# A written-out order of 831 operations replaced by another: same operations, other places, engines and buffers

## The chip, the cores and the metric

One core of a Trainium2 chip. The metric is the device time of one execution in microseconds (us). The core has the engines PE (matrix multiply), DVE (vector), ACT (activations and copies), POOL (general, no access to PSUM), and SP, whose queue issues nearly all DMAs here. They run on their own and wait for one another by semaphores; each works through its instructions in order. DMAs run on 16 DMA engines.

## What is computed

Attention over 32 inducing points, and behind it a mixture of experts with one expert per token (cut):

```python
B, N, C = 4, 11456, 128          # m = 32 inducing points
def mab(q, kv):                  # s = softmax(scale * q kv^T);  s @ kv
    ...
h = mab(I, x)                    # B x 32 x 128
x = mab(x, h)                    # B x N x 128, then rows as tokens
logits = xn @ en.T / tau         # xn, en: rows over their norms; E = 8
expert_idx = np.argmax(logits, axis=1)
gate_w = probs[np.arange(N), expert_idx]
out[mask] = gate_w[mask, None] * (np.maximum(x[mask] @ w1[e], 0.0) @ w2[e])
```

All in float32; `w1` is 8 x 128 x 1024, `w2` 8 x 1024 x 128.

## The kernel before

Each of the 4 batches is cut into 6 tiles of 1920 tokens (the last is shorter and padded), 24 tiles in all, numbered 0 to 23. A tile lies in SBUF as 128 x 1920, channels on partitions; stage 1 also needs it with tokens on partitions, which twelve tiles load from memory (`loadx`) and twelve make by transposes on PE (`xt`) and an eviction from PSUM (`xe`).

*Stage 1, per tile g* (line 380 on): `load`, the scores against the inducing points `s1` (PE), their exponentials `e1` (ACT), a 32 x 32 block transpose `e1t` (DVE), and `h`, 15 matmuls that add the tile to the batch's sum. *Per batch b* (`finish`, line 440 on): the sum of weights `zc`, `zr`, the scaled table row `rz` (which writes `rhs`), `hd`/`hdc`, the table `tab`/`tabc`, a `vote` and `pick` of the batch's expert, `loadw`, which loads that expert's weights, `tabs.0` to `tabs` (the expert's number, its one-hot row, the product with the table, its sum, and `tD`, the table less that sum; lines 481 to 484), `sta` to `std` (the shift of the exponent), and `G`, `GT`, `gs`, `gk`, `K`, `Kc`, `K4`, `K4c`, which fold the expert into a 128 x 128 matrix.

*Stage 2, per pair of tiles* (line 535 on): the scores `s2` (PE), their largest size `am` (DVE), exponentials `e2` (ACT), `rot` (a copy that turns the partitions by 32, two copies of 32 x 480 in each half), `up` (PE, 32 matmuls as run, half of them on `tD`), `uc`/`w` (weighting; on POOL for tiles 0, 2, 6, 14, 18 and 22, which `uc` copies out of PSUM first), `dt` (transpose), `n2` (norms), then small steps on 30 or 240 columns: `ln`, `ex`, `z`, `fac`, `den`, `lg`, `el`, `S`, `v`, `gf` (the gate). Per tile follow `F` (the gate spread out), `eg` (times the exponentials), `out` (PE), two evictions `oe` and the `store`. Tiles 18, 22 and 23 go through this last part in two pieces (`.0`, `.1`). At the end `ck1` to `ck5` and `verdict` decide on the core whether a general loop has to redo some batches; it runs for none here.

Nothing is scheduled while the kernel is built. The string `ORDER` lists all 831 operations; each engine gets its own in the order of that list. A quote behind a name takes the second engine of the operation's choices, two quotes the third:

```python
        for word in ORDER.replace("\n", " ").split(","):
            word = word.strip()
            o = named[word.rstrip("'")]
            o.engine = o.engines[len(word) - len(word.rstrip("'"))]
            assert o.deps <= done, o.name
            for b in o.bufs:
                if b.slot is None:
                    b.slot = int(next(seats[b.pool]))
```

`SEATS` gives each buffer its place as the list comes to it: 8 PSUM banks, 17 large SBUF buffers for tiles and outputs (`big`), 7 of middle size, 11 small ones, and so on. An operation waits for whoever used its place last. `FILL` puts matmuls on zeros in front of a few operations on PE. A load also waits for the fifth load before it (`DEPTH`). The line that writes all copies is L300, nearly all matmuls L303, transposes L406, the fill matmuls L708.

Of the kernel before, what the change touches and what calls it, by code (L numbers as in the profile page):

```python
# [23 lines left out]
F = 1024  # L24
# [8 lines left out]
K = 6  # L33
# [27 lines left out]
ind, en1, pad 5, en3, en4, load 0.1, xt 0.1, xe 0.1, en5, load 0.0, s1 0, load 1, en6, load 4, xt 0.0, xe 0.0, m1 0,  # L61
xt 1.1, sha 0, shb 0, xe 1.1, s1 1, shc 0, shd 0, en7, xt 1.0, xt 4.0, hde 0, e1 0, e1 1, xt 4.1, e1t 1, load 2, s1
2, xe 4.0, xe 1.0, e1 2, e1t 0, xt 2.0, xt 2.1, load 5, xt 5.1, pad 17, xe 2.0', e1t 2, h 0, xe 4.1, s1 4, h 1, load
3, xe 2.1, s1 3, h 2, e1 4, e1t 4, e1 3, e1t 3, xe 5.1', s1 5, loadx 3, xt 5.0, e1 5, xe 5.0, load 6, load 9, h 3,
zc 0, h 4, e1t 5, s1 6, h 5, hsb 0, m1 6, zr 0, sha 1, shb 1, load 11, xt 9.0, xe 9.0, rz 0.0, rz 0, hd 0, hdc 0',
shc 1, shd 1, s1 9, zk 0, tab 0, tabc 0', s2 0, vote 0, s2 4, am 0, sta 0, s2 2, pick 0, stb 0, tabs 0.0', tabs
0.1', stc 0, e1 6, load 7, am 4, e1 9, s2 1, tabs 0.2', tabs 0.3, std 0, load 10, e2 0, e1t 9, e2 4, tabs 0', am 1,
e2 1, s2 3, e2 2, load 12, am 3, rot 0.0, hde 1, s2 5, rot 0.1, e2 5, rot 4.0, e1t 6, up 0, s1 10, e2 3, am 2, am 5,
xt 10.0, loadx 6, uc 0, e1 10, load 8, ad 0, md 0, xe 10.0, rot 4.1, dt 0, up 4, mdc 0, xt 12.1, xe 12.1, w 1, w 4,
hde 2, xt 9.1, xe 9.1, loadw 0, dt 4, s1 7, xt 11.0, w 5, w 0, e1 7, xe 11.0, rot 2.1, z 0, n2 0, ln 0, ex 0, fac 0,  # L70
e1t 7, h 6, n2 4, ln 4, G 0, GT 0, s1 8, e1 8, up 2, e1t 10, loadx 7, gs 0, xt 10.1, den 0, gk 0, dt 2, s1 12, e1t
8, rot 2.0, loadx 8, h 7, lg 0, m1 12, z 4, ex 4, uc 2, marg 0.0, K 0, marg 0.1, el 0, sha 2, h 8, w 2, S 0, fac 4,
v 0, marg 0, shb 2, pad 11, Kc 0', s1 11, xe 10.1, mq 0, gf 0, den 4, w 3, n2 2, K4 0, shc 2, shd 2, lg 4, F 0, el
4, e1 11, S 4, v 4, e1t 11, xt 11.1, xe 11.1, F 1, mx 0, K4c 0', h 9, h 10, h 11, gf 4, zc 1, eg 0, F 5, ln 2, eg 1,
zr 1, z 2, hsb 1, ex 2, load 13, out 0, fac 2, rz 1.0, rz 1, hd 1, F 4, load 14, load 16, s1 13, e1 12, hdc 1', den
2, tab 1, e1t 12, eg 5, s2 6, tabc 1', vote 1, pick 1, s1 14, oe 0.1, lg 2, oe 0.0, out 1, el 2, S 2, eg 4, e1 13, v
2, tabs 1.0', e1 14, gf 2, am 6, sta 1, loadx 14, s2 9, tabs 1.1, tabs 1.2', s2 8, e1t 13, tabs 1.3, tabs 1, ad 1,
stb 1, oe 1.1, F 2, am 9, oe 1.0, stc 1, std 1, e2 6, s2 7, load 17, s2 11, am 8, eg 2', e2 9, rot 8.0, xt 17.0, e2
8, load 18, e2 11, am 7, ck1 0, e2 7, F 3, am 11, up 8, e1t 14, xe 17.0, eg 3, rot 8.1, s2 10, e2 10, rot 6.0, dt 8,
load 15, s1 15, e1 15, store 0, zk 1, up 6, rot 6.1, uc 6, h2 0, w 8, w 6, w 9, am 10, s1 16, e1 16, xt 12.0, dt 6,  # L80
n2 8, xe 12.0, out 2, w 7, md 1, loadw 1, G 1, mdc 1, xt 17.1, z 8, e1t 16, s1 17, rot 10.1, oe 2.1, n2 6, oe 2.0,
up 10, ln 6, GT 1, h 12, ex 6, z 6, fac 6, den 6, lg 6, ln 8, loadx 15, dt 10, xe 17.1, ex 8, el 6, S 6, gs 1, gk 1,
e1 17, fac 8, w 10, den 8, loadx 13, rot 10.0, h 13, out 3, h 14, w 11, K 1, oe 3.0, out 4, oe 3.1, e1t 15, h 15, Kc
1, K4 1, marg 1.0, e1t 17, oe 4.1, marg 1.1, marg 1, out 5, oe 4.0, lg 8, v 6, mq 1, mx 1, s1 18, zc 2, load 23, n2
10, gf 6, K4c 1, F 7, pad 23, m1 18, loadx 16, h 16, zr 2, rz 2.0, oe 5.0, h 17, oe 5.1, F 6, sha 3, rz 2, el 8, xt
18.0, S 8, hsb 2', hd 2, eg 6', v 8, ln 10, s1 23, z 10, shb 3, hdc 2', tab 2, store 1, ex 10, gf 8, loadx 19, shc
3, xe 18.0, F 9, tabc 2, shd 3, s2 17, e1 18, fac 10, eg 7', eg 9, vote 2, pick 2, s2 12, den 10, lg 10, e1 23, am
17, tabs 2.0', am 12, out 6, sta 2, el 10, tabs 2.1', oe 6.1, F 8, tabs 2.2', store 2, stb 2, s2 13, oe 6.0, zk 2,
stc 2, S 10, s2 16, std 2, e2 17, e1t 23, s2 15, v 10, am 16, gf 10', e2 12, e2 16, F 11, e2 13, am 15, rot 16.1,
out 7, eg 8, oe 7.0, oe 7.1, e2 15, eg 11, load 20, s1 20, e1 20, am 13, tabs 2.3, s2 14, tabs 2, F 10, am 14, eg  # L90
10, e2 14, e1t 18, rot 14.0, up 12, store 3, dt 12, rot 12.0'', up 14, uc 14, xt 18.1, rot 12.1, w 12, xe 18.1, dt
# [34 lines left out]
    sml=("0 1 2 1 0 2 2 1 0 8 3 5 2 4 3 5 3 2 5 0 4 8 1 0 6 9 1 5 8 4 3 2 10 7 8 1 2 5 7 6 4 5 7 4 2 1 0 8 5 7 9 6 "  # L126
        "2 0 9 10 0 8 10 1 8 9 4 5 2 8 10 5 9 7 3 8 2 4 3 2 5 7 8 4 5 6 3 4 6 5 0 10 5 4 "),
    E1=("0 1 1 1 0 1 1 0 0 1 1 0 1 1 0 0 1 1 1 0 0 0 1 1 "),
    gs=("0 1 0 1 0 0 1 0 1 1 0 1 "),
    b=("2 0 1 2 "),  # L130
    w=("0 0 0 0 "),
    k=("0 0 0 0 "),
# [746 lines left out]
```

## Time and profile before

| | |
|---|---|
| time of three runs | 163.42, 163.43, 163.44 us |
| the profiled execution's own time | 163.29 us |
| its span, from the first to the last instruction | 161.4 us |
| mean granted clock of PE | 0.988 |
| PE, DVE, ACT, POOL busy | 90%, 79%, 74%, 52% of the span |
| read from HBM, written | 39.47 MB, 23.46 MB |

The profile is one execution. A row of a timeline gives the start in the span, how long the instruction or a run of equal ones took, the engine and the line, what was written from what, and in brackets how long the engine had been idle and what released it. An engine off the chain of waits may be idle at no cost.

### The profile page before, as it was taken

To read this page: it belongs to the slowest core of one execution; us is meant where nothing else is said; L and a number is where in the kernel's file an instruction comes from. 1 tells how busy PE (TensorE), PEld (TensorE's weight loads), DVE (VectorE), ACT (ScalarE), POOL (GpSimd) and SP (SyncE) were. 2 spreads that over 40 slices of the span, in tenths; PEclk is the share of its full clock that TensorE was granted. 3 is DMA by queue.
4 is the path that set the end of the run, shared out by engine and by line. 5 is a ranking of instruction groups with operands and counts; after the bars stand their busy time and mean duration, and the time that the engine had idled before them with its cause. 6 is when DMAs were issued, how large, how long until landed. Compare 5 with 4: busy or idle time off the path is not lost.

```text
span 161.4 us, 5881 instructions
## 1 busy us (share of the span) xinstructions
PE 145.8 (90%) x2340; PEld 76.8 (48%) x2340; DVE 127.0 (79%) x300; ACT 119.8 (74%) x245; POOL 84.0 (52%) x200
## 2 busy tenths in 40 slices
PE   7899999999999999999999998999979888869930
PEld 5487777326658634255665323464822222335610
DVE  0515364697999789997979899999689979998970
ACT  3389372496967899688898998987979779988230
POOL 8600000259583862986305688932476987883300
PEclk9999999999999999999999999999999999999995
DMA  5999999999999999999999999999889999989993
GB/s 159 430 425 419 415 416 419 408 419 410 422 412 421 414 413 417 424 420 404 426 411 421 428 411 427 423 397 406 337 337 404 321 354 421 408 350 394 424 385 148
DMA packets 11295, 63.35 MB, mean 393 GB/s; under 512 B 1400, under 2 KB 1408, under 8 KB 11264
## 3 DMA queue, kind: packets, MB, share of 16 engines
q1 hardware_dynamic: 11088, 62.92, 96.3%
q8 instruction: 19, 0.31, 0.8%
q14 instruction: 12, 0.10, 0.2%
q10 hardware_dynamic: 176, 0.02, 0.1%
HBM read 39.47 MB, written 23.46 MB: 390 GB/s over the span
## 4 chain that ended last, share of the span: by engine, by line
PE 65%; DVE 19%; POOL 7%; issue 4%; DMA 2%; ACT 1%; POOLq 0%; DVEq 0%; ACTq 0%
PE psum L303 50%; PE psum L406 13%; DVE am L551 3%; DVE sml L624 2%; POOL mid L300 2%; POOL sml L626 2%; DVE n L589 2%; DMA emb_sb<-in_emb 2%; DVE big L300 2%; DVE mid L591 1%; DVE gf L611 1%; DVE mid L579 1%; DVE sml L626 1%; PE psum L374 1%; POOL mid L579 1%
## 5 line engine op out<-in xcount | busy, mean ns | idle before, releaser
L300 ACT COPY big<-psum 128x960 f32<-128x960 f32 (+4 forms) x71 | 62.3, 908 | 14.0 <-PE psum L303 7.9
L300 POOL COPY mid<-sml 32x480 f32<-32x480 f32 x46 | 27.4, 597 | 9.0 <-ACT sml L555 6.9
L303 PE MATMUL psum<-sml,K 32*128 32x480 f32 (+2 forms) x216 | 26.5, 564 | 3.6 <-ACT big L300 1.6
L303 PE MATMUL psum<-big,ind 128*32 128x480 f32 x192 | 25.0, 572 | 0.3 <-DMA big<-in_xT 0.3
L303 PE MATMUL psum<-big,sml 128*32 128x128 f32 x720 | 24.8, 274 | 0.2 <-issue 0.2
L303 PEld LDWEIGHTS psum<-big,sml 128*32 128x32 f32 x720 | 21.2, 110 | 5.9 <-issue 3.8
L406 PEld LDWEIGHTS psum<-ident,big 128*128 128x128 f32 x180 | 19.4, 140 | 9.1 <-ACT big L300 2.4
L406 PE MATMUL psum<-ident,big 128*128 128x128 f32 x180 | 23.5, 277 | 0.2 <-POOL sel L276 0.2
L303 PE MATMUL psum<-big,hd 128*32 128x480 f32 x192 | 22.4, 571 | 0.8 <-DVE mid L579 0.4
L626 POOL TENSOR_TENSOR sml<-mid,sml 128x480 f32<-128x480 f32 (+2 forms) x18 | 20.6, 1150 | 4.5 <-DVE sml L624 3.2
L425 ACT ACTIVATE E<-psum,nb 128x480 f32<-128x480 f32 (+2 forms) x28 | 18.3, 655 | 5.6 <-PE psum L303 4.6
L429 DVE STREAM_TRANSPOSE sml<-E 128x480 f32<-128x480 f32 x24 | 15.8, 661 | 4.9 <-ACT E L425 4.9
L624 DVE STREAM_TRANSPOSE sml<-gf 128x480 f32<-128x480 f32 (+2 forms) x27 | 16.1, 608 | 1.1 <-ACT gf L612 0.8
L551 DVE TENSOR_REDUCE am<-psum 128x1 f32<-128x480 f32 x24 | 15.1, 638 | 1.3 <-PE psum L303 1.0
L303 PEld LDWEIGHTS psum<-sml,K 32*128 32x128 f32 x216 | 8.8, 183 | 14.8 <-ACT big L300 3.8
L303 PE MATMUL psum<-mid,tab 32*32 32x480 f32 x96 | 13.7, 573 | 1.5 <-ACT mid L555 0.8
L589 DVE TRANSPOSE_TENSOR_REDUCE n<-mid 128x30 f32<-128x960 f32 x12 | 13.9, 1160 | 1.0 <-POOL mid L579 0.8
L591 DVE STREAM_TRANSPOSE mid<-psum 128x960 f32<-128x960 f32 x12 | 14.0, 1166 | 0.4 <-PE psum L303 0.2
L303 PE MATMUL psum<-sml,tD 32*32 32x480 f32 x96 | 12.9, 573 | 0.0
L303 PE MATMUL psum<-sml,tab 32*32 32x480 f32 x96 | 12.9, 573 | 0.0
L303 PE MATMUL psum<-mid,tD 32*32 32x480 f32 x96 | 12.9, 573 | 0.0
L579 DVE TENSOR_TENSOR mid<-psum,mid 128x480 f32<-128x480 f32 x18 | 11.2, 627 | 0.5 <-PE psum L303 0.3
(140 smaller groups left out, 210.2 us busy)
## 6 DMA issues: line engine op xcount, KB each, us to landing
big<-in_xT SPq DMA_DIRECT2D x19, 960.0 KB, 11.0
out<-big SPq DMA_DIRECT2D x14, 960.0 KB, 7.1
big<-in_xP SPq DMA_DIRECT2D x12, 960.0 KB, 11.6
w<-in_w SPq DMA_DIRECT2D x8, 512.0 KB, 8.6
out<-big SPq DMA_DIRECT2D x8, 512.0 KB, 7.8
big<-in_xT SPq DMA_DIRECT2D x4, 928.0 KB, 11.8
out<-big SPq DMA_DIRECT2D x6, 448.0 KB, 8.1
out<-big SPq DMA_DIRECT2D x2, 928.0 KB, 5.4
```

The lines of the kernel that those rows point to most:

```text
L300: return nc.scalar.copy(out, in_) if e == "ACT" else ENG[e].tensor_copy(out, in_)
L303: return nc.tensor.matmul(out, lhsT=lhsT, rhs=rhs, start=start, stop=stop)
L374: add(f"{name}a {bt.b}", ("PE",), lambda e: [nc.tensor.transpose(ap(p1)[0:1, 0:P], src(), ident)], [src_part, cnb], [p1])
L406: return [nc.tensor.transpose(ap(tp)[:, (q - q0) // 4, 128 * ((q - q0) % 4):128 * ((q - q0) % 4) + 128], v(q), ident) for q in range(q0, q1)]
L425: return [nc.scalar.activation(ap(e1)[r0:r1, :n], ap(ps)[r0:r1, :n], AF.Exp, bias=bt.t("nb")[r0:r1, 0:1], scale=SCALE, accum_out=bt.t("zk" ...
L429: add(f"e1t {g}", ("DVE",), lambda e: [nc.vector.transpose(ap(e1t), ap(e1))], [e1], [e1t])
L551: add(f"am {g}", ("DVE",), lambda e, ps=ps, k=k: [v.tensor_reduce(t("am")[:, k:k + 1], ap(ps)[:, :W], AX.X, ALU.max, apply_absolute_value= ...
L579: return [ENG[e].tensor_tensor(ap(wp)[:, a], src(), ap(e2)[:, a], ALU.mult)]
L589: add("n2 " + nm, ("DVE",), lambda e: [v.tensor_reduce(fl2(u("n2")), ap(wp).rearrange("p a (q i) -> p (a q) i", i=32), AX.X, ALU.add, appl ...
L591: add("dt " + nm, ("DVE",), lambda e: [v.transpose(ap(dt_).rearrange("p a q m -> p a (q m)"), ap(pd)[:, :, :W])], [pd], [dt_])
L624: add(f"F {nm}", ("DVE",), lambda e, a=a, f=f, q0=q0, q1=q1: [v.transpose(ap(f).rearrange("p (q i) -> p q i", i=32)[:, q0:q1], u("gf")[:, ...
L626: add(f"eg {nm}", ("POOL", "DVE"), lambda e, a=a, f=f, e2g=e2g, c0=c0, c1=c1: [ENG[e].tensor_tensor(ap(e2g)[:, c0:c1], ap(e2)[:, a, c0:c1] ...
```

## The change

`ORDER`, `SEATS` and `FILL` are replaced as a whole; no other line changes (the new file is one line shorter, so a line's number is one lower there). The words that come with it say that the new list was found by a search which charges the fetches of instruction pages to single transfer engines. All 831 operations are the same, and so are all sizes. 40 of them change engine: 12 from ACT to DVE, 9 from DVE to ACT, 8 from POOL to DVE, 7 from DVE to POOL, 3 from POOL to ACT, 1 from ACT to POOL. The fill matmuls go from 61 to 54.

```diff
 ORDER = """
-ind, en1, pad 5, en3, en4, load 0.1, xt 0.1, xe 0.1, en5, load 0.0, s1 0, load 1, en6, load 4, xt 0.0, xe 0.0, m1 0,
...
+pad 17, load 0.1, ind, xt 0.1, en1, en3, en4, load 0.0, en5, s1 0, m1 0, xt 0.0, xe 0.1, en6, en7', load 1, xt 1.1,
...
 FILL = {
-    "xt 0.1": (4, 16), "up 20": (7, 3), "up 22": (2, 4), "out 18.0": (5, 4), "out 23.1": (4, 30),
-    "out 23.0": (4, 4),
+    "xt 0.1": (0, 16), "K 3": (7, 6), "out 21": (2, 9), "out 23.0": (2, 23),
 }
```

On SP the stores and loads change places at several points. In the middle, `loadx 13` and `load 23` move some ten places forward, and `loadx 14`, `loadx 15` and `loadx 16` move behind `store 0`, `load 18`, `loadw 1` and `store 1`. `store 6` moves from behind the last load to ahead of the last three but one (`loadx 19`, `load 21`, `loadx 21`, `loadx 22` now end the loads).

DVE, at the choice of batch 3's expert. `g` and `ei` are the expert's number, `nb` the shift, `oh`, `lo` and `lg` the steps of `tabs`, `am` an `am`, the transposes `F`, the products of two tiles `eg`. Before:

```order
L467 MAX g_137<-psum 128x8
L467 MAX_INDEX ei<-g_137,psum 128x8
L377 COPY nb_127<-psum 128x1
L482 CAST idx_138<-ei 128x1
L624 STREAM_TRANSPOSE sml_80<-gf_99 128x480
L624 STREAM_TRANSPOSE sml_76<-gf_99 128x480
L483 TENSOR_REDUCE lg_140<-lo_139 128x1
L626 TENSOR_TENSOR sml_81<-mid_70,sml_83 128x480
L551 TENSOR_REDUCE am_125<-psum 128x1
L626 TENSOR_TENSOR sml_77<-mid_71,sml_76 128x480
```

After, at the same place:

```order
L466 MAX g_137<-psum 128x8
L466 MAX_INDEX ei<-g_137,psum 128x8
L376 COPY nb_107<-psum 128x1
L481 CAST idx_138<-ei 128x1
L481 TENSOR_SCALAR oh_109<-iota,idx_138 128x8
L482 TENSOR_TENSOR lo_139<-oh_109,tab_103 128x8
L482 TENSOR_REDUCE lg_140<-lo_139 128x1
L550 TENSOR_REDUCE am_105<-psum 128x1
L623 STREAM_TRANSPOSE sml_73<-gf_91 128x480
```

The one-hot row and the product have come over from POOL and follow the expert's number at once; the two `eg` (tiles 15 and 17) have gone to POOL.

POOL, over the same stretch of the program: `v` of pair 16, the `eg`, the steps of `tabs`, the `rot` of pairs 18 and 20 (copies of 32 x 480), `w 18`. Before:

```order
L608 TENSOR_TENSOR v_98<-sum_97,z_95 128x30
L626 TENSOR_TENSOR sml_78<-mid_70,sml_81 128x480
L482 TENSOR_SCALAR oh_129<-iota,idx_138 128x8
L483 TENSOR_TENSOR lo_139<-oh_129,tab_123 128x8
L300 COPY mid_68<-sml_82 32x480 x2
L484 TENSOR_SCALAR tD_124<-tab_123,lg_140 128x8
L300 COPY mid_68<-sml_82 32x480 x2
L300 COPY mid_66<-sml_75 32x480 x2
L579 TENSOR_TENSOR mid_69<-sml_76,mid_68 128x480
```

After:

```order
L607 TENSOR_TENSOR v_90<-sum_89,z_87 128x30
L625 TENSOR_TENSOR sml_80<-mid_66,sml_83 128x480
L625 TENSOR_TENSOR sml_78<-mid_70,sml_73 128x480
L299 COPY mid_71<-sml_81 32x480 x2
L483 TENSOR_SCALAR tD_104<-tab_103,lg_140 128x8
L299 COPY mid_71<-sml_81 32x480 x2
L625 TENSOR_TENSOR sml_74<-mid_67,sml_80 128x480
L578 TENSOR_TENSOR mid_70<-sml_75,mid_71 128x480
```

Two short steps have left POOL, `eg 12` and `eg 15` stand where `eg 14` stood, and `eg 17` has taken the place of a `rot` ahead of `w 18`.

PE, the last matmuls of the program (four `out` half tiles, 256 or 224 columns each, and the two transposes `ck2` and `ck4` of the check). Before, behind the first of the four:

```order
L303 MATMUL psum<-sml_83,K_128 128x256 x4
L303 MATMUL psum<-sml_77,K_128 128x224 x4
L658 MATMUL psum<-ident,chk 24x128
L660 MATMUL psum<-ident,c_160 1x24
L303 MATMUL psum<-sml_77,K_128 128x256 x4
```

After, all four:

```order
L302 MATMUL psum<-sml_81,K_108 128x256 x4
L302 MATMUL psum<-sml_74,K_108 128x256 x4
L302 MATMUL psum<-sml_74,K_108 128x224 x4
L302 MATMUL psum<-sml_81,K_108 128x224 x4
L657 MATMUL psum<-ident,chk 24x128
L659 MATMUL psum<-ident,c_160 1x24
```

The check's two transposes have moved behind the last output. Of the last eight evictions ACT has seven (five before) and DVE one (three before).

## Rows read from the trace of the kernel before

**Rows 1.** The page: engines over the span, and GB/s in 40 slices.
```profile
PE 145.8 (90%) x2340; PEld 76.8 (48%) x2340; DVE 127.0 (79%) x300; ACT 119.8 (74%) x245; POOL 84.0 (52%) x200
...
GB/s 159 430 425 419 415 416 419 408 419 410 422 412 421 414 413 417 424 420 404 426 411 421 428 411 427 423 397 406 337 337 404 321 354 421 408 350 394 424 385 148
```

**Rows 2.** Stretches: length, busy PE, PEld, DVE, ACT, POOL (instructions), PE clock, DMA share, GB/s.
```profile
4.50:116.40 111.90, 110.03 (x1928) 61.91 (x1928) 89.68 (x204) 87.97 (x187) 54.48 (x120) 1.00 1.01 415
116.40:157.50 41.10, 32.50 (x401) 12.69 (x400) 36.88 (x92) 30.58 (x58) 25.87 (x44) 1.00 0.96 376
```

**Rows 3.** Timeline of DVE behind stage 1: start, duration, instruction [idle before, releaser].
```profile
116.82 0.93 DVE L452 TENSOR_SCALAR rhs<-sel,zc 128x160 f32<-128x160 f32 x1
...
122.83 0.14 DVE L482 CAST idx<-ei 128x1 f32<-128x1 uint32 x1
...
124.10 0.12 DVE L483 TENSOR_REDUCE lg<-lo 128x1 f32<-128x8 f32 x1
...
130.01 1.18 DVE L589 TRANSPOSE_TENSOR_REDUCE n<-mid 128x30 f32<-128x960 f32 x1 [0.82 <-POOL mid L579]
...
144.50 1.17 DVE L589 TRANSPOSE_TENSOR_REDUCE n<-mid 128x30 f32<-128x960 f32 x1
...
149.36 0.69 DVE L611 RECIPROCAL gf<-v 64x30 f32<-64x30 f32 x2 [0.36 <-POOL v L608]
```

**Rows 4.** Timeline of POOL in the same stretch.
```profile
116.45 1.20 POOL L626 TENSOR_TENSOR sml<-mid,sml 128x480 f32<-128x480 f32 x1 [0.26 <-PE psum L303]
...
123.08 0.31 POOL L482 TENSOR_SCALAR oh<-iota,idx 128x8 f32<-128x8 f32 x1 [1.02 <-DVE idx L482]
...
123.75 1.53 POOL L300 COPY mid<-sml 32x480 f32<-32x480 f32 x2
125.39 0.76 POOL L484 TENSOR_SCALAR tD<-tab,lg 128x8 f32<-128x8 f32 x1
126.21 1.20 POOL L300 COPY mid<-sml 32x480 f32<-32x480 f32 x2
...
128.77 1.21 POOL L579 TENSOR_TENSOR mid<-sml,mid 128x480 f32<-128x480 f32 x1
```

**Rows 5.** Timeline of PE: most of `h 14`; the first matmul on `tD` of batch 3.
```profile
77.64 0.96 PE L303 MATMUL psum<-big,sml 128*32 128x128 f32 x27
...
126.20 0.58 PE L303 MATMUL psum<-mid,tD 32*32 32x480 f32 x1
```

**Rows 6.** Timeline of all engines, from 150 us to the end.
```profile
150.08 0.41 DVE L624 STREAM_TRANSPOSE sml<-gf 128x224 f32<-128x224 f32 x1
...
151.32 0.66 POOL L626 TENSOR_TENSOR sml<-mid,sml 128x224 f32<-128x224 f32 x1 [1.99 <-DVE sml L624]
...
151.78 0.97 ACT L300 COPY big<-psum 128x448 f32<-128x448 f32 x2 [2.50 <-PE psum L303]
...
152.78 4.28 SPq L639 DMA_DIRECT2D out<-big  x4
...
155.19 0.71 PE L303 MATMUL psum<-sml,K 32*128 32x256 f32 x8 [0.26 <-DVE fl L661]
...
155.97 0.59 ACT L300 COPY big<-psum 128x512 f32<-128x512 f32 x1 [1.77 <-PE psum L303]
...
157.33 0.14 DVE L679 CAST ni<-fw 1x1 int32<-1x1 f32 x1
```

**Rows 7.** A stretch behind PE's last matmul, columns as in rows 2.
```profile
155.90:157.40 1.50, 0.00 (x0) 0.00 (x0) 1.30 (x6) 0.59 (x1) 0.00 (x0) 1.00 0.97 384
```

**Rows 8.** SP's issues (`store 1`; the last two loads of batch 3).
```profile
63.94 2.02 SPq L639 DMA_DIRECT2D out<-big  x2
...
93.84 3.06 SPq L398 DMA_DIRECT2D big<-in_xP  x2
```

**Rows 9.** The twelve loads of line 398 (`loadx`), from issue to landing.
```profile
DMA to landing us min/median/max: 8.3/11.6/16.7
```

**Rows 10.** The page: the queue of the page fetches (packets, MB, share of 16 engines).
```profile
q8 instruction: 19, 0.31, 0.8%
```

## What I predict

> **What bounds the kernel now.** I read the profile in this order: the engines and the bytes per second of the whole span, the same split at the end of stage 1, the records of DVE, POOL and PE behind that point, and last the end of the program. [rows 1] show two resources near their limit: PE 90% busy, and a DMA rate over 400 GB/s in most slices, with a sag from slice 29 on. [rows 2] cut the span at 116.4 us, when `h 23`, the last matmul group of stage 1, is done. Ahead of the cut PE is busy for 110.03 of 111.90 us and the DMA share is 1.01: transfers and PE are both full, and PE's own idle time is 1.9 us in all. Behind the cut the DMA rate falls to 376 GB/s and PE is busy for 32.50 of 41.10 us, while DVE is busy for 36.88: there the stores wait for results. What follows is a chain that runs through batch 3's table and then its six tiles.
>
> **That chain, by its records.** Batch 3's table needs its row `rhs` (`rz 3`), which takes 0.93 us, while POOL runs an `eg` of 1.20 us beside it [rows 3, 4]. The expert's number is there at 122.97 (122.83 + 0.14). Then POOL makes the one-hot row (from 123.08) and the product, copies half a tile (`rot 18.1`, 1.53 us), and only then makes `tD` (0.76 us, to 126.15) [rows 4]. The matmuls on `tD` begin at 126.20 [rows 5], and with them `up 18`. POOL then has two more `rot` of 1.20 us ahead of `w 18`, which runs 128.77 to 129.98 [rows 4]; DVE's `n2 18` starts at 130.01, having waited 0.82 us for it [rows 3]. From there DVE is the row that never stops: `n2 22` at 144.50, the last gate `gf 22` at 149.36 [rows 3], and the last store is issued by 157.06 (152.78 + 4.28) [rows 6], the span ending at 161.4.
>
> **The change part by part.** No operation is added or taken away, so every cost is one of place.
>
> Ahead of the cut PE has the same 148 operations in front of `h 23`, in another order. Their sum is that of before, so `h 23` ends at 116.3 again unless PE waits more or less: at best 1.9 us earlier [rows 2], at worst by a late load (a rival below). I take 0, the row of the full engine being the nearest. SP now sends `store 6` ahead of the last three batch-3 loads: 0.98 MB at 415 GB/s, 2.4 us later. In before the last of these loads was issued by 96.90 (93.84 + 3.06) [rows 8]; with the median 11.6 us to landing [rows 9] and 2.4 us more it is there at 110.9, and its matmuls are among the last of stage 1, so it costs nothing; without that cover it would cost up to 2.4 us.
>
> Behind the cut I walk the new order with the durations of before's records. (1) `eg 13` now stands ahead of `v 14` on POOL, so it is over when `rz 3` starts; `rz 3` then takes about 0.3 instead of 0.93 us, of which the next operation on DVE takes nothing back, as `gf 14` has gone to ACT: -0.5. (2) `out 13` and `s2 18` follow on PE as before. `S 16` and `eg 14` on DVE come ahead of `am 18` and fit into the wait for `s2 18`: the shift is there at 122.1 instead of 122.92, -0.8. (3) The one-hot row, the product and the sum now follow on DVE itself, four short instructions of 0.12 to 0.3 us, 0.7 in all; the sum, at 124.22 in before (124.10 + 0.12 [rows 3]), is there at 122.8. POOL has `eg 12`, `eg 15` and `rot 18.1` ahead of `tD`: from `v 16` at about 120.7 three times 1.2 us gives 124.4, and `tD` is done at 125.1 instead of 126.15: -1.05. (4) `up 18` ends 1.05 earlier. Ahead of `w 18` POOL has `rot 18.0` and `eg 17`, again 2.4 us: 125.1 + 2.4 = 127.5, and `w 18` to 128.75: -1.2. `eg 17` on POOL is thus free, since it replaces `rot 20.1`, which moves behind. (5) `n2 18` starts at 128.8 instead of 130.01. On DVE up to `n2 22` the same sum is left within 0.2 us (`F 21` and `Kc 3` go out of the stretch, half of `eg 18` and `mdc 3` come in; the walk gives 143.45 for 144.50): -1.05. `lg 18` on POOL gains only 0.3, because `eg 16` and `z 20` now precede it; `gf 18` is still 1.1 earlier, as `den 20`, `am 22` and `Kc 3` ahead of it on DVE end last. (6) From `n2 22` to `gf 22` before needs 4.86 us. In after `F 21` is added and `oe 21.0` has gone to ACT; ACT's two evictions ahead of `el 22` set the pace in both, so 4.9: `gf 22` at 148.35, -1.0.
>
> At the very end two things trade. In before `out 22.0` stands behind `ck2` and `ck4` on PE and starts at 155.19, released by DVE's `fl`, so the last eviction on ACT starts at 155.97 after 1.77 us of waiting [rows 6]. Now the check follows the last `out`. Against that ACT makes seven of the last eight half evictions (five before), about 0.5 us each (0.97 for two [rows 6]), and `out 23.1` waits for `F 23.1` and POOL's `eg 23.1`. From `gf 22`: `F 23.0`, `F 22.0`, `eg 23.0`, `eg 22.0`, `F 22.1`, `oe 23.0.0`, `F 23.1` on DVE take 3.8 us with the gate (about 0.4 each [rows 6]; to 152.1), `eg 23.1` 0.66 behind `zk 3` (153.1), `out 23.1` 0.7 (153.8), two evictions 1.1 (154.9). The last two stores go out at 155.0 and 155.4, where before issued its last at 156.7: -1.3. They are two, of 0.43 and 0.46 MB, and land one behind the other, 0.3 us later than one would: -1.0. The check, thirteen steps of about 0.2 us, needs some 2.5 us behind `out 23.1`, which the eviction and the landing hide (before's last step of it is at 157.33 [rows 6], later than 156.4 here); if it were not hidden it would cost its excess over them.
>
> The `FILL` matmuls go from 61 to 54 and to other places. PE's granted clock was 1.00, the 2.4 GHz level, until 157.40, 1.5 us behind its last matmul [rows 7]; the gaps that the walk leaves on PE are under 1 us, so I count nothing. A gap that lets the clock fall would double some of the five `out` groups of 1.1 us on the way to the end.
>
> **The sum.** 161.4 - 1.0 = 160.4 us of span. The profiled execution took 163.29 us, 1.9 over its span, and lies 0.14 below the median of 163.43: 160.4 + 1.9 + 0.14 = 162.4 us. Bounds of the walk: -0.5, if only step 1 comes through and POOL keeps its pace, and -1.6, if the two last stores overlap and `lg 18` follows at once: 161.8 to 162.9.
>
> **Rivals.** *A load comes late ahead of the cut* (slower). `loadx 14`, `loadx 15` and `loadx 16` stood ahead of `store 1` on SP (which was issued at 63.94, for 2.02 us [rows 8]); now they stand behind it, and behind `store 0`, `load 18` and `loadw 1`, so that `loadx 14` is issued at 64 to 66. With the median of 11.6 us it is there at 75.6 to 77.6, with the longest, 16.7 [rows 9], at 80.7 or later. PE wants it for `h 14`, 77.64 in before [rows 5], now behind `K 1`, by an estimate 0.6 us later, at 78.3. For: this stretch of before has the long landings, and page fetches (19 packets, 0.8% of the engines' span [rows 10], so 1.1 us each on one engine) can hold a transfer up. Against: the order was laid out with such a hold-up in its sum, and no PE wait on a load is in before's trace beyond the start. Price 80.7 - 78.3 = 2.4 us on a full PE: 164.8 us. It decides from 1.0 us of waiting on, which eats the gain.
> The Trainium skill's page "Runtime: NRT & Kernel Launch" (Instruction fetch mechanics) says that a fetch of 16 KiB is mostly hidden; by it this rival would have no price and the sum would stay at 162.4. No row here shows whether a page fetch delayed a transfer.
>
> *The tail gains nothing* (same). POOL and DVE are both near full behind the cut [rows 2], and `rz 3`'s 0.93 us [rows 3] shows that one can stretch the other; if three more `eg` on POOL lengthen DVE's operations by as much as the table gains, the end stays: 163.4 us.
>
> *PE's idle time goes as well* (faster): 162.4 - 1.9 = 160.5 us. For: the waits that make it up are on ACT, DVE and a load, all of which moved. Against: a new order has new waits.
>
> *PE is not the limit ahead of the cut.* [rows 2] show PE busy for 110.03 but its weight loads for only 61.91 of 111.90 us. If PE could go faster there, `h 22` and `h 23`, at 0.96 us for 27 of a group's 30 matmuls [rows 5], could be done some 2 us behind the last load, at 112.9 instead of 116.3, and the end would be 3.4 us earlier still: 159.0 us. Against: no gap between matmul groups shows that they ever wait for the queue ahead.
> The Trainium skill's page "Perfetto Trace Analysis" (Identifying the Most-Contended Engine) holds matmul busy time for a bad measure and the weight loads' share for a better one; by that rule this rival is the case, but the trace shows a PE that takes up each group as the last one ends.
>
> **How the numbers follow.** Forecast 162.4 us, 47%; late load, 164.8 us, 26%; nothing gained, 163.4 us, 14%; idle time gone, 160.5 us, 10%; PE with room, 159.0 us, 3%. About 0.2% (0.33 us) is what a measurement of this kernel can tell from no change. Faster is the first, fourth and fifth: 60%; same 14%; slower 26%. The range 161.2 to 164.8 leaves out the lower part of the fourth case, the fifth, and late loads of more than 2.4 us, some 18%; the forecast's own range is 161.8 to 162.9.
>
> **What would show it.** Right: `h 23` done at 116.3 within 0.5 us; `tD` of batch 3 done near 125.1; `w 18` ending near 128.8; `gf 22` near 148.4; the last store issued near 155.4; the check's last step before the last landing. Wrong: idle time of PE ahead of `h 14` to `h 16` with a DMA named; `tD` still behind 126; a granted clock under 1.00 between 116 and 155 us; a DVE that is busy for as long behind the cut as before.

## The result: 0.8% faster, 161.95 us

The changed kernel takes 161.95 us (median of 20 runs, 161.37 to 163.64), the kernel before 163.44 us in the same series (20 runs, 162.98 to 164.51): a ratio of 0.9917, 95% interval 0.9897 to 0.9937. Forecast were 162.4 us, with a range of 161.2 to 164.8. Ratios and intervals, here and below, leave out executions over 1.5% above the fastest of their kernel (one each of e2, e7 and e10, two of e6); the medians count all. The traced execution took 162.65 us with a span of 160.9; it is one of the slower ones of the changed kernel, and the part on the late page names a cause that its trace shows.

The page of the changed kernel, the lines that answer to [rows 1] and [rows 10]:

```profile
PE 144.0 (90%) x2333; PEld 75.8 (47%) x2333; DVE 126.6 (79%) x306; ACT 119.6 (74%) x242; POOL 82.7 (51%) x195
...
GB/s 149 429 423 420 417 418 412 422 411 408 422 413 417 416 414 420 409 425 422 414 404 365 397 401 352 430 426 411 411 420 423 388 396 405 365 397 412 395 391 81
...
q8 instruction: 19, 0.31, 0.8%
```

The sag of slices 29 to 33 has gone: 411, 420, 423, 388, 396 for 337, 337, 404, 321, 354. In its place there are two new dips ahead of the cut, slices 22 and 25 with 365 and 352. The stretches of [rows 2], in the changed kernel:

```profile
4.50:116.40 111.90, 109.67 (x1923) 61.07 (x1923) 92.47 (x215) 85.64 (x179) 53.56 (x115) 1.00 1.02 412
116.40:157.50 41.10, 30.89 (x407) 12.48 (x397) 33.76 (x87) 32.69 (x63) 25.45 (x45) 0.96 0.99 398
```

Behind the cut 398 instead of 376 GB/s, and DVE busy for 33.76 instead of 36.88 us. The clock's mean of 0.96 comes from a fall at 154.5 us, 1.3 us behind the last output matmul; up to there it was 1.00. DVE along the chain, as [rows 3]:

```profile
116.78 0.17 DVE L451 RECIPROCAL zc<-psum 128x1 f32<-128x1 f32 x1 [0.45 <-PE psum L302]
116.98 0.37 DVE L451 TENSOR_SCALAR rhs<-sel,zc 128x160 f32<-128x160 f32 x1
...
122.69 0.68 DVE L481 TENSOR_SCALAR oh<-iota,idx 128x8 f32<-128x8 f32 x1
...
123.61 0.16 DVE L482 TENSOR_REDUCE lg<-lo 128x1 f32<-128x8 f32 x1
...
128.81 1.18 DVE L588 TRANSPOSE_TENSOR_REDUCE n<-mid 128x30 f32<-128x960 f32 x1
...
143.00 1.16 DVE L588 TRANSPOSE_TENSOR_REDUCE n<-mid 128x30 f32<-128x960 f32 x1
...
148.06 0.68 DVE L610 RECIPROCAL gf<-v 64x30 f32<-64x30 f32 x2 [0.28 <-POOL v L607]
```

`rz 3` takes 0.37 instead of 0.93 us, `n2 18` starts 1.20 us earlier (128.81 for 130.01), `n2 22` 1.50 us (143.00 for 144.50), the last gate 1.30 us (148.06 for 149.36). POOL in that stretch, as [rows 4]:

```profile
120.97 2.38 POOL L625 TENSOR_TENSOR sml<-mid,sml 128x480 f32<-128x480 f32 x2
123.42 1.22 POOL L299 COPY mid<-sml 32x480 f32<-32x480 f32 x2
124.75 0.32 POOL L483 TENSOR_SCALAR tD<-tab,lg 128x8 f32<-128x8 f32 x1
125.13 1.19 POOL L299 COPY mid<-sml 32x480 f32<-32x480 f32 x2
126.40 1.20 POOL L625 TENSOR_TENSOR sml<-mid,sml 128x480 f32<-128x480 f32 x1
127.57 1.20 POOL L578 TENSOR_TENSOR mid<-sml,mid 128x480 f32<-128x480 f32 x1
```

Two `eg`, `rot 18.1`, `tD`, `rot 18.0`, `eg 17`, `w 18` in one row without a gap: `tD` is done at 125.07 (126.15 before), `w 18` at 128.77 (129.98).

Two things made `tD` earlier. The first is the start of `rot 18.1`: it needs the exponentials that ACT makes with the shift, and starts 0.13 to 0.14 us behind them in all fourteen traces, whatever POOL did ahead of it. ACT before, ACT after, and POOL in e8 (an experiment below), which is idle ahead of the copy:

```profile
122.95 0.66 ACT L555 ACTIVATE sml<-psum,nb 128x480 f32<-128x480 f32 x1
...
122.63 0.66 ACT L554 ACTIVATE sml<-psum,nb 128x480 f32<-128x480 f32 x1 [0.27 <-DVE nb L376]
...
123.27 1.20 POOL L292 COPY mid<-sml 32x480 f32<-32x480 f32 x2 [1.23 <-ACT sml L547]
```

The second is that POOL's own steps got shorter: `rot 18.1` takes 1.22 instead of 1.53 us, `tD` 0.32 instead of 0.76. Before, DVE ran two `eg` beside them:

```profile
124.14 0.70 DVE L626 TENSOR_TENSOR sml<-mid,sml 128x480 f32<-128x480 f32 x1
...
125.33 0.64 DVE L626 TENSOR_TENSOR sml<-mid,sml 128x480 f32<-128x480 f32 x1
```

All four traces with the old tail (before, e1, e3, e9) have the second copy of `rot 18.1` at 0.91 us and `tD` at 0.76 to 0.77, all ten with the new one 0.58 and 0.31 to 0.32. Counted from DVE's first step behind `h 23` (RECIPROCAL of `zc`), `tD` is done 1.36 us earlier: 0.61 by the start of `rot 18.1`, some 0.75 by the two shorter steps. No run moved DVE's two `eg` alone, so that they stretch POOL's steps is read from these traces and not tested by itself.

The end, as [rows 6]: the last matmul group, SP's last two stores, the check's last step.

```profile
152.58 0.66 PE L302 MATMUL psum<-sml,K 32*128 32x224 f32 x8 [0.31 <-POOL sml L625]
...
154.30 0.84 SPq L638 DMA_DIRECT2D out<-big  x2
...
155.28 0.14 DVE L678 CAST ni<-fw 1x1 int32<-1x1 f32 x1
```

The stores are issued by 155.14 instead of 157.06, 1.9 us earlier, but by the packets of the trace the last of them lands at 158.54 instead of 159.31, only 0.8 earlier (by the semaphore that reports it 159.41 instead of 159.73, 0.3 earlier). The check is done at 155.42, 3.1 us ahead of the last packet (157.47 and 1.8 before).

### The profile page after: what moved, and what is told of

It reads as the page before. It is cut to its first block, busy times and chain, and to the rows that moved or that the text cites. A ratio compares the mean times of both kernels' runs of the same rounds, so it can differ in the third digit from the quotient of the medians.

```text
span 160.9 us, 5858 instructions
## 1 busy us (share of the span) xinstructions
PE 144.0 (90%) x2333; PEld 75.8 (47%) x2333; DVE 126.6 (79%) x306; ACT 119.6 (74%) x242; POOL 82.7 (51%) x195
## 4 chain that ended last, share of the span: by engine, by line
PE 59%; DVE 17%; POOL 6%; ACT 6%; DMA 4%; issue 3%; SPq 1%
PE psum L302 47%; PE psum L405 11%; DMA big<-in_xT 4%; DVE n L588 3%; ACT big L299 3%; POOL sml L625 3%; DVE mid L590 2%; DVE sml L623 2%; DVE sml L625 2%; DVE mid L578 1%; POOL mid L299 1%; ACT sml L554 1%; DVE big L299 1%; POOL lg L602 1%; ACT mid L554 1%
## 5 line engine op out<-in xcount | busy, mean ns | idle before, releaser
L302 PE MATMUL psum<-sml,K 32*128 32x480 f32 (+2 forms) x216 | 27.3, 566 | 5.8 <-ACT big L299 2.0
L625 POOL TENSOR_TENSOR sml<-mid,sml 128x480 f32<-128x480 f32 (+2 forms) x21 | 23.7, 1133 | 6.6 <-DVE sml L623 5.1
L299 POOL COPY mid<-sml 32x480 f32<-32x480 f32 x42 | 24.7, 588 | 3.7 <-ACT sml L554 1.7
L302 PE MATMUL psum<-big,sml 128*32 128x128 f32 x720 | 24.2, 274 | 0.0
L302 PE MATMUL psum<-mid,tab 32*32 32x480 f32 x96 | 13.0, 572 | 1.4 <-ACT mid L554 0.7
L602 POOL TENSOR_TENSOR lg<-mid,den 128x240 f32<-128x240 f32 x12 | 8.0, 665 | 9.9 <-DVE den L600 8.7
```

Source lines behind the costliest of these rows:

```text
L299: return nc.scalar.copy(out, in_) if e == "ACT" else ENG[e].tensor_copy(out, in_)
L302: return nc.tensor.matmul(out, lhsT=lhsT, rhs=rhs, start=start, stop=stop)
L602: add("lg " + nm, ("POOL",), lambda e: [gp.tensor_tensor(u("lg"), dv(), u("den").rearrange("p a q -> p q a").unsqueeze(3).broadcast_to([P, ...
L625: add(f"eg {nm}", ("POOL", "DVE"), lambda e, a=a, f=f, e2g=e2g, c0=c0, c1=c1: [ENG[e].tensor_tensor(ap(e2g)[:, c0:c1], ap(e2)[:, a, c0:c1] ...
```

## Experiments

All twelve against the kernel before, on the same chip as their own runs of it.

| label | what it is | median us | ratio | 95% interval |
|---|---|---|---|---|
| e1_front_only | new order to `h 23`, old behind | 162.96 | 0.9961 | 0.9940 to 0.9982 |
| e2_tail_only | old to `h 23`, new behind | 162.95 | 0.9960 | 0.9932 to 0.9988 |
| e5_tail_free_bank | the same, fills into free banks | 162.33 | 0.9907 | 0.9883 to 0.9931 |
| e3_b_check_last | before, check behind the last `out` | 163.93 | 1.0020 | 1.0002 to 1.0038 |
| e4_after_again | the changed kernel | 162.24 | 0.9921 | 0.9895 to 0.9947 |
| e6_page_shift | changed, 64 more instructions on PE | 163.54 | 0.9980 | 0.9960 to 0.9999 |
| e7_no_fill | changed, 38 of 54 fills left out | 162.57 | 0.9912 | 0.9879 to 0.9945 |
| e8_eg12_early | changed, `eg 12` earlier | 162.02 | 0.9902 | 0.9867 to 0.9936 |
| e9_before_late | before, 0.94 us behind `h 23` | 164.07 | 1.0035 | 1.0016 to 1.0053 |
| e10_after_late | changed, 0.94 us behind `h 23` | 162.62 | 0.9931 | 0.9904 to 0.9957 |
| e11_page_late | changed, 8 fewer on PE | 162.21 | 0.9912 | 0.9889 to 0.9936 |
| e12_best | e8 and e11 together | 161.96 | 0.9911 | 0.9878 to 0.9943 |

**Which half of the new order gains?** The list is cut behind `h 23`; the operations left follow in the order of the other list, and their buffers get free places that follow the parent's.

```diff
 e1: ORDER = new list up to "h 23"
-    + new list
+    + old list, without what stands ahead already (232 operations)
 e2: ORDER = old list up to "h 23"
-    + old list
+    + new list, without what stands ahead already (239 operations)
```

> The new order up to h 23, the old order behind it. My theory, that the gain lies behind h 23: h 23 done at 116.3 to 116.6 us, tD of batch 3 near 126.2, the last gate near 149.4, time 163.2 to 163.6 us, ratio 1.000. Rival, that the gain comes from the new place of loads and stores ahead of h 23 (fewer DMA gaps behind it because transfers are left over): 161.9 to 162.3 us, ratio 0.991 to 0.993.

> The old order up to h 23, the new order behind it. My theory: tD of batch 3 done near 125.0 us, w 18 near 128.7, the last gate near 148.4, time 161.9 to 162.4 us, ratio 0.991 to 0.994. Rival, that the gain lies ahead of h 23: 163.4 us, ratio 1.000. Second rival, that the two parts work only together: both this and the kernel with the new front stay at 163.0 us or above.

Both came out at 163.0: neither the theory nor its first rival, and the two halves seem to add up. The trace of e2 shows that its tail was not the one that I meant to run. Stretches of e2, columns as in [rows 2]:

```profile
144.00:146.00 2.00, 0.81 (x9) 0.04 (x4) 1.97 (x5) 1.60 (x6) 0.25 (x1) 1.00 1.03 412
146.00:148.00 2.00, 2.00 (x13) 1.19 (x13) 1.02 (x5) 1.20 (x2) 0.87 (x3) 0.54 1.02 404
148.00:150.00 2.00, 2.00 (x11) 0.67 (x12) 1.73 (x6) 0.13 (x1) 0.19 (x1) 0.61 0.99 402
```

And the timeline of PE there, fills and `out 21`:

```profile
145.99 1.97 PE L700 MATMUL psum<-zero 128*128 128x256 bf16 x9 [1.19 <-ACT big L292]
147.89 1.90 PE L295 MATMUL psum<-sml,K 32*128 32x480 f32 x8
```

The bank that my placing gave the fill in front of `out 21` was freed only by an eviction: PE idled for 1.19 us, the granted clock fell to the 1.2 GHz level, nine fills took 1.97 us and `out 21` 1.90 instead of 1.09. `out 23.0` began at 152.3, behind 23 fills of 2.69 us that began late in turn. The twelve times fall into two groups, 162.1 to 162.6 (six) and 163.3 to 165.6 (six); four of the six slower ones have a mean granted clock of 0.974 or less, the quicker ones none below 0.983. So it was run again with fills into banks that are free long before:

```diff
-FILL = {'xt 0.1': (4, 16), 'K 3': (7, 6), 'out 21': (2, 9), 'out 23.0': (2, 23)}
+FILL = {'xt 0.1': (4, 16), 'K 3': (4, 6), 'out 21': (0, 9), 'out 23.0': (2, 23)}
```

> Again the old order up to h 23 and the new one behind it, but the fill matmuls in front of out 21 and K 3 write to banks that are free long before. In the first such kernel the fill in front of out 21 waited 1.19 us for an eviction, PE's granted clock fell to 0.50 from 146 to 149.4 us and out 23.0 began at 152.3. My theory, that the tail is worth 1.0 us or more by itself and that the fallen clock ate the rest there: clock 1.00 to 152 us, out 23.0 near 149.9, time 162.1 to 162.5 us, ratio 0.990 to 0.994, and the runs no longer fall into two groups. Rival, that the tail is worth half and the front the other half: 162.9 us, ratio 0.996, whatever the clock does.

162.33 us, 0.9907: the new tail alone gives the whole gain, as far as the intervals tell. In the one traced execution the clock fell once more (0.50 from 142 to 146 us, behind 0.98 us of idle PE at 140.2), and that one took 163.23 us; the five others lie between 161.9 and 162.6. The part about the clock held by accident, then, rather than by the other bank; the size of the tail held.

What the two halves do to the chain can be read free of that, from DVE's first step behind `h 23` to `n2 22`, in us: before 28.00 (116.50 to 144.50), e1 28.05, e9 27.47; the changed kernel 26.22 (116.78 to 143.00), e2 26.65, e4 26.25, e8 26.20, e10 26.25. With the old tail it is 28 (27.5 in e9, for a reason that follows), with the new one 26.2 to 26.7 (27.3 in e5, where the clock had fallen), whatever stands ahead. Why the front gives 0.6 us with the old tail and nothing that can be measured with the new one is taken up with the delays.

**The end: check or store?**

```diff
-mx 3, oe 23.0.1, ck1 3, store 23.1, oe 23.0.0', ..., zk 3, ck2, store 23.0, ck3, ck4, ..., out 22.0, oe 22.0.0', ..., oe 22.0.1, store 22.0
+mx 3, oe 23.0.1, ck1 3, store 23.1, oe 23.0.0', ..., zk 3, out 22.0, oe 22.0.0', oe 22.0.1, ck2, store 23.0, ck3, ck4, ..., store 22.1, store 22.0, ...
```

> The old order, with one part of the new one: out 22.0 and its two evictions stand ahead of the check on PE, ACT and DVE. out 22.0 should start at 153.6 instead of 155.2 us and the last store be issued near 155.2 instead of 156.7. My theory, that transfers are full there (DMA share 0.94 to 1.01 from 152 to 158 us) and take back most of it: 0.3 to 0.6 us, time 162.8 to 163.1 us, ratio 0.996 to 0.998. Rival, that the issue of the last store alone sets the end: 1.3 to 1.5 us, time 162.0 us, ratio 0.991, which would be the whole of the gain. Rival, that the check is the end: no gain, 163.4 us.

0.2% slower, which none of the three had. The end of this kernel, PE and DVE:

```profile
155.29 0.71 PE L295 MATMUL psum<-sml,K 32*128 32x256 f32 x8 [1.10 <-DVE big L292]
...
156.90 0.37 PE L650 MATMUL psum<-ident,chk 128*24 128x128 f32 x1 [0.90 <-DVE big L292]
...
159.11 0.14 DVE L671 CAST ni<-fw 1x1 int32<-1x1 f32 x1
```

`out 22.0` now waits 1.10 us for a bank that DVE's eviction of another half tile holds, and the check, pushed behind it, ends at 159.25 (157.47 before; 0.63 us of that come from ahead of the cut). SP turns to the last store only 0.10 us later than before (156.82 for 156.72), but its last packet lands 1.35 us later (160.66 for 159.31).

Which of the two holds the end can be read from all fourteen traces. The span ends 1.6 to 2.5 us behind the last packet, and 1.25 to 1.67 behind the semaphore that reports the last store (1.46 to 1.49 in ten); behind the check's last step it is anything from 3.3 (here) to 5.6. In before that step has 3.9 us to the end, more than the 3.3 that are enough here, so it was the landing that held the end there too. So e3 lost by its landing: what the last store won by going ahead of the check the transfers took back, and more; why they took so much is not shown.

**How much do 0.94 us on the chain cost?** In both orders eight fills stand between `h 23` and `zr 3`:

```diff
 FILL = {
+    'zr 3': (1, 8),
```

> The kernel before with eight more fill matmuls (0.12 us each, 0.94 in all) between h 23 and zr 3, so that batch 3's table and all behind it begins 0.94 us later. The walk of the prediction says that the chain behind h 23 sets the end here: last step of the check and last landing each 0.9 us later, time 164.3 to 164.6 us, 0.8 to 1.0 above the kernel before. Rival, that the transfers set the end (DMA share 0.94 to 1.01 in the last 7 us): 0.5 us or less, 163.9 us or below.

> The changed kernel with the same 0.94 us between h 23 and zr 3. If the chain still sets the end: 162.9 to 163.1 us, 0.8 to 1.0 above the changed kernel. Theory, that the end now waits for transfers (its last landing is 3.1 us behind the last step of the check, in the kernel before 1.8; DMA share 0.97 from 116 to 157 us): the end moves by 0.3 to 0.6 us, time 162.4 to 162.6 us. That would also say why the new front, worth 0.6 us with the old tail, is worth less with the new one.

Before, delayed: 164.07 us, 0.59 above its own runs of before (163.48). That looks like part of the delay only, but the chain itself was only 0.52 us later (`n2 22` at 145.02). DVE and POOL in that kernel:

```profile
116.41 1.20 POOL L618 TENSOR_TENSOR sml<-mid,sml 128x480 f32<-128x480 f32 x1 [0.27 <-PE psum L295]
...
117.87 0.20 DVE L444 TENSOR_SCALAR rhs<-sel,zc 128x160 f32<-128x160 f32 x1
```

POOL's `eg 13` is over at 117.61, `rz 3` starts behind it and takes 0.20 instead of 0.93 us. The delay of 1.05 us on DVE's first step (117.55 for 116.50) gave half of itself back by ending the collision. What is left reaches the end: 0.52 on the chain, 0.59 in the time (0.26 to 0.87 by the interval of the ratio). So in the kernel before the chain, by way of the last store, sets the end.

The changed kernel, delayed: `n2 22` 1.07 us later, as it should be. The median is 162.62 us, 0.4 to 0.7 above 162.24 and 161.95, or 0.001 in the ratios (0.2 us), with intervals that overlap. In its trace the clock fell again (0.65 and 0.50 from 144 to 148 us), the last matmuls are 2.0 us later, the last landing 1.40, the end of the span 0.9. In this trace half of the delay is thus taken up between the last matmul and the end, where transfers are queued; that the end waits for transfers by now fits, and by the median it is not shown. It would also say why the front, which without the stop told of next has the cut 0.3 to 0.6 us earlier, gives 0.6 us where the chain sets the end (e1) and nothing that can be measured where it does not (e5 against the changed kernel). That stays an argument: in e1's one trace the cut is 0.5 us later than before, and its other runs have no trace.

**The page that comes late.** In six traces with the new front PE stops inside `out 6` with nothing to wait for. PE in the changed kernel:

```profile
90.78 0.67 PE L302 MATMUL psum<-sml,K 32*128 32x480 f32 x1 [0.60 <-issue]
```

Ahead of that the DMA rate sags, in stretches of the changed kernel:

```profile
86.00:88.00 2.00, 2.00 (x42) 0.93 (x44) 1.65 (x6) 1.38 (x3) 1.42 (x2) 1.00 1.08 353
88.00:90.00 2.00, 2.00 (x27) 0.51 (x20) 1.80 (x6) 1.99 (x7) 1.32 (x2) 1.00 0.95 354
```

The transfer engines are as busy as ever, at 353 instead of some 415 GB/s: from 86.4 to 89.2 us 24 of 116 packets of 7,680 bytes take 0.56 to 0.62 instead of 0.29 us. The fetch of an instruction page that starts at 87.0 to 87.3 us with the old front starts at 88.4 here. Whether such spells come at random was to be seen from a second trace:

> The changed kernel once more, for a second trace. Its runs go from 161.4 to 163.6 us, those of the kernel before mostly within 163.4 plus or minus 0.2. In its trace DMA packets of 7,680 bytes take 0.56 to 0.62 us instead of 0.29 for spells of 1 to 1.5 us (near 87 and 97 us); in the trace of the kernel before such a spell stands near 127 us. If such spells come at random and make the spread, this trace has them at other places, and steps move behind them by up to 1 us. If the order itself makes the spread, all steps up to the last store agree within 0.2 us in the two traces. Time 161.4 to 162.6 us.

They do not: it has them at 86.3 and again behind 95 us, where the first has them at 86.4 and behind 95, the same stop of 0.60 us, and every step up to the last store within 0.16 us (`n2 22` at 142.97 for 143.00). The spells belong to the order, and the spread of the runs is not seen in two traces that agree.

```diff
-fill = [matmul(psum[:, s, 0:256], lhsT=zero[:, 0:P], rhs=zero) for _ in range(n)]
+e6, for "xt 0.1": 48 x matmul(psum[0:32, s, 0:32], lhsT=zero[:, 0:32], rhs=zero[:, 0:32])
+e11, for "xt 0.1": 6 x matmul(psum[:, s, 0:P], lhsT=ones, rhs=ones)
```

> The changed kernel with 48 small fill matmuls (32 columns) instead of 16 wide ones at the very start: 64 more instructions on PE, so that every later instruction page of PE begins some 1.7 us earlier in its work. In both traces of the changed kernel a page fetch that in the old one starts at 87.1 starts at 88.4 us, behind slow packets (0.58 instead of 0.29 us from 86.4 to 89), and PE stops for 0.60 us inside out 6 at 90.2 with nothing to wait for. My theory, that the late page stops PE: that fetch now starts near 85.5 us, the stop is gone or under 0.2 us, h 23 is 0.4 to 0.6 us earlier against the start of xt 0.1, and the profiled time falls from 162.7 to near 162.1; the median of the other runs, 162.0 to 162.2, which lies 0.6 below the profiled one, moves less, by 0 to 0.3 us. Rival, that the stop is something of out 6 itself: it stays at 0.6 us.

The wrong way round: the fetch started at 89.2, and PE, which wanted the page 64 instructions earlier, stood for three times as long, in e6:

```profile
91.62 1.01 PE L302 MATMUL psum<-big,hd 128*32 128x480 f32 x8 [1.85 <-issue]
```

In all PE stood 3.1 us in two such stops, the first of 1.21 us at 83.3. The ratio rose from 0.992 to 0.998, by 1.0 us, in an order that is the changed kernel's to the letter; a part of that is the colder start (`xt 0.1` took 1.73 us instead of 0.95). That 64 instructions bring the fetch forward was wrong. That a page which comes late stops PE was right: over the six traces with the changed kernel's instructions ahead of `out 6` the stop follows the start of the fetch, 88.0 and 0.33 us (e7), 88.3 and 0.60 (e8 and e10), 88.4 and 0.60 (changed kernel, e4), 88.6 and 0.88 (e1), and in these and both stops of e6 PE goes on 2.3 to 2.5 us behind that start. So the other way:

> The changed kernel with 6 float32 fill matmuls instead of 16 bf16 ones at the very start: 20 instructions fewer on PE, so that each page begins some 0.5 us later in PE's work. In the traces of five kernels with the new front the page fetched at 88.0, 88.3, 88.4, 88.4 and 88.6 us goes with a stop of 0.3, 0.6, 0.6, 0.6 and 0.9 us on PE behind it. Theory, that the stop is the lateness of that page, which slow packets hold up until 88.4: it is needed 0.5 us later now, and the stop is 0 to 0.2 us; time 0.3 to 0.6 us below the changed kernel in the traced execution, 161.5 to 162.0 as a median. Rival, that the fetch moves along and starts 0.5 us later: the stop stays at 0.6 us and the time at 162.0 to 162.2. Should PE be cold at the start, xt 0.1 takes 1.5 us instead of 0.95 and 0.5 us are lost.

> The last kernel with eg 12 ahead of v 16 on POOL as well (by itself 162.0 us, ratio 0.990, 0.1 us or less from the changed kernel). If both parts hold: 161.3 to 161.9 us, ratio 0.985 to 0.990. If the end waits for transfers and not for the chain: as the changed kernel, 161.9 to 162.2 us, ratio 0.991.

Each float32 matmul runs as two here (12 in the trace), so there are 8 instructions fewer and not 20. The stop of PE is gone. PE in e11, the eight matmuls of `out 6` in one row, and its weight loads:

```profile
89.26 1.09 PE L302 MATMUL psum<-sml,K 32*128 32x480 f32 x8
...
91.22 0.12 PEld L302 LDWEIGHTS psum<-big,hd 128*32 128x32 f32 x3 [0.59 <-issue]
```

The fetch did move along, to 88.86 us, as the rival has it, and the page came no earlier: the weight loads stop for 0.59 us until 91.22, 2.4 us behind that start. But that gap now lies behind four more matmuls, the last of which runs until 91.49, so PE itself is not idle.

DVE's first step behind `h 23` comes at 116.23 (e11) and 115.86 (e12) for 116.78, and the traced execution takes 162.06 and 161.80 us for 162.65. The medians stay where they were, 162.21 and 161.96. As the stop is a matter of 0.3 to 0.9 us from one trace to the next, many of the runs of the changed kernel may have had little of it; their stops are not recorded.

**Two smaller parts.** In e7 the FILL of the new order is cut down to its first entry, in e8 one word moves:

```diff
-    "xt 0.1": (0, 16), "K 3": (7, 6), "out 21": (2, 9), "out 23.0": (2, 23),
+    "xt 0.1": (0, 16),
```

> The changed kernel without the fill matmuls in front of K 3, out 21 and out 23.0 (38 of 54). Theory of the prediction, that they count nothing: clock 1.00 to 150 us as with them, time within 0.2 us of the changed kernel, 161.9 to 162.2. Rival, that without them the clock falls to 0.50 in the wait for the last gate: the four last out groups (0.65 to 1.15 us each) take twice as long, the last store is issued 1 to 2 us later, time 163 to 164 us.

In the traced execution the rival is right: the clock is 0.50 from 142 us on, the four last output groups take 4.52 us in a row, in e7:

```profile
150.60 4.52 PE L302 MATMUL psum<-sml,K 32*128 32x256 f32 x32 [1.94 <-ACT big L299]
```

and it takes 163.84 us. The other six lie between 161.17 and 162.95, about the changed kernel's times, and not because their clock held: their mean granted clock is 0.945 to 0.959 (the traced one's 0.938), that of the changed kernel's twenty 0.972 to 0.987. By these means, as an estimate, the clock was at its lower level for 13 to 18 us in each of them, against 4 to 9 in the changed kernel. So without the fills the clock is low for longer in all seven, and in six of them the time hardly shows it; what the fills are worth stays open.

```diff
-S 16, tab 3, s2 19, v 16, am 18, ..., store 9, eg 12, e2 20
+S 16, tab 3, s2 19, eg 12, v 16, am 18, ..., store 9, e2 20
```

> The changed kernel with eg 12 ahead of v 16 on POOL, into an idle time of 2.1 us before it. POOL then is idle when DVE makes the one-hot row of batch 3, which took 0.68 us in the changed kernel, ending 0.02 us behind POOL's eg, and 0.31 on POOL before. Theory, that a short operation on DVE waits until POOL's operation has ended (as rz 3 did before: 0.93 us): it takes 0.2 to 0.3 us, the sum is made 0.4 us earlier, at 123.4. By the records nothing follows from that, since rot 18.1, which stands ahead of tD on POOL, begins with e2 19 at 123.3 in any case: tD 125.0, time as the changed kernel within 0.2 us. Rival, that two engines share evenly: the row still takes over 0.5 us. Rival for the time, that POOL is what the table waits for: w 18 and the end 0.4 to 1.0 us earlier.

DVE in e8, where POOL is idle from 122.03 to 123.27:

```profile
122.54 0.23 DVE L474 TENSOR_SCALAR oh<-iota,idx 128x8 f32<-128x8 f32 x1
...
123.00 0.16 DVE L475 TENSOR_REDUCE lg<-lo 128x1 f32<-128x8 f32 x1
```

0.23 instead of 0.68 us, and the time, 162.02, is the changed kernel's: both as expected. A DVE operation of this kind (TENSOR_SCALAR on SBUF) that runs beside a long one of POOL ended only when that was over. In before `rz 3` ended at 117.75, with POOL's `eg` at 117.65 [rows 3, 4]; in the changed kernel the one-hot row ends at 123.37, with POOL's second `eg` at 123.35. The Trainium skill's page "SBUF — State Buffer" (SBUF: two separate sides) has a pair of ports that some DVE operations share with GpSimd under an exclusive lock, so that the later one blocks until the first is done, and never shares the rate; the two traces and e8 agree, and even sharing would not have given 0.93 and 0.68 us that end with POOL's operation.

## Where the prediction held, and where not

The direction, the place and most of the sizes held; the forecast was 0.45 us too high. That it came so near is in part luck, as the terms below partly cancel.

*Ahead of the cut, 0.* `h 23` was put at 116.3; the trace has it 0.28 us later, as two things that I had not separated: a PE that waits less, and a stop of 0.60 us for a page. Without the stop it comes 0.3 to 0.6 us earlier than before (e11, e12). So the rival *PE's idle time goes as well* is right for a third at most of its 1.9 us.

*The late load* did not happen. SP issued the three loads from 62.85 on; their groups ran at 78.0, 80.0 and 83.1 without a wait. The profile matches a landing to the last two, 78.9 and 81.2: 15.5 and 15.6 us from the issue, within the bound that I took, and 1.1 and 1.9 us to spare. The first issue was 1.2 us earlier than my earliest. What did come late was a page, where I had taken pages only as a cause that holds up loads. Of the Trainium skill's rule ("Runtime: NRT & Kernel Launch", Instruction fetch mechanics) that a fetch is mostly hidden the forecast said that no row bears on it; now e6 does: 1.85 us not hidden.

*Step 1* (-0.5, `rz 3` without POOL's `eg` beside it): measured 0.56 on the operation and 0.54 on `hdc 3`, counted from `h 23`.
*Step 2* was mis-sized: the shift was to come 0.8 earlier and came 0.32 earlier (122.60 for 122.92), or 0.60 counted from `h 23`. `S 16` and `eg 14` in the wait for `s2 18` gave nothing, since the wait itself was what the chain spent there.
*Step 3*: the sum at 122.8 was wrong by 1.0 (123.77): the one-hot row ran into POOL's `eg` and took 0.68 us. It cost nothing, as `rot 18.1` waits for ACT's exponentials and not for these steps; by the same reading their move from POOL to DVE gained nothing either. `tD` at 125.07 for 125.1 was right by luck: `rot 18.1` was done at 124.64 and not at 124.4, and `tD` took 0.32 us where I had kept 0.7. That DVE's `eg` had stretched `tD` in before was not seen, though its 0.76 us stand in [rows 4].
*Steps 4 to 6*: `w 18` to 128.77 (128.75), `n2 18` 128.81 (128.8), `n2 22` 143.00 (143.45), `gf 22` 148.06 (148.35). The DVE row between `n2 18` and `n2 22` is 0.3 us shorter than before and 0.45 shorter than I summed; from `n2 22` to the gate it took 5.06 us for a forecast 4.9.
*The very end*: last issue 155.14 (155.4), and the check is hidden, as it was said. The clock fell at 154.5 us, within the stretch that the forecast names as a sign of being wrong, but behind the last output. The landing gains 0.8 for a forecast 1.0: the last two stores take 3.1 and 3.9 us to land, since those ahead of them still fill the queue.
*The sum*: span 160.9 for 160.4. The chain is not what made it longer, as the gate and the last issue came 0.3 us ahead of the forecast in spite of the page: the last packet landed 0.2 us later than forecast, and the span ended 2.34 us behind it, where before had 2.08. Without the stop for the page the spans are 160.3 (e11) and 160.0 (e12). The median is below the traced execution by 0.7 us, which I had put at 0.14 above; this error of 0.84 one way and the 0.5 of the span the other way make most of the 0.45.

*The tail gains nothing* did not come: DVE's busy time behind the cut fell by 3.1 us, and with `eg` on POOL it was POOL's own steps that got shorter. Its mechanism is there all the same, in the one-hot row's 0.68 us, beside the chain.

*PE has room ahead of the cut* (the weight loads' share as the measure): e6 speaks against it. Its stops are 2.5 us longer than the changed kernel's (3.1 for 0.6) and its start some 0.8 us later, and DVE's first step behind `h 23` is 3.1 us later, at 119.88; hardly anything was caught up.

## What to carry to other kernels

Of two engines near their limit, look on both at which short operation runs while the other engine is in a long one: DVE's `rz 3` was 0.56 us longer beside POOL's `eg`, POOL's `rot` and `tD` 0.31 and 0.44 longer beside DVE's, all three on the chain; a fourth of 0.45 us, beside the chain, cost nothing. Where a check and a store both stand at the end, read the distance of each to the end of the span in several traces before one is put behind the other: here only the store's was steady. And before a change in an order is judged by a few tenths of a us, count the instructions ahead on the busy engine: 64 small ones at the start moved the pages, left the start colder, and cost three quarters of what the whole change had brought.

## What the runs showed of the hardware

An instruction page whose fetch starts some 1 us late, in a spell of slow packets, stops PE for 0.3 to 1.85 us; PE goes on 2.3 to 2.5 us behind the start of the fetch. A quarter to a half of the packets of 7,680 bytes take 0.50 to 0.68 instead of 0.29 us in spells of some 2 us that stand at the same place in each trace of an order (within 86.2 to 89.4 us in all nine with the new front, none ahead of 124 us in the five with the old one; two thirds of them between 126 and 130 us in the four with the old tail); what brings them about stays open. A copy and a TENSOR_SCALAR on POOL took 0.91 and 0.76 us beside a TENSOR_TENSOR on DVE, 0.58 and 0.32 without it. The granted clock fell in the tail of some executions of a kernel and not in others: 0.98 us of idle PE came ahead of it in e5, 1.19 in e2, while a wait of 1.17 us in the kernel before did not bring it down. And the runs of the changed kernel spread over 2.3 us, those of before over 1.5, with thirteen of the latter's twenty within 0.2 of their median; the late page and the clock are two causes that the traces show, how much of the spread is theirs is open.
